# GpSimd raises a constant to a power for 19 score tiles, with the first pair in row order and the final adds on GpSimd

## Chip, cores, metric

One core of a Trainium2 chip. The metric is device microseconds of one execution. Engines are written as in the profile: PE is TensorE, PEld its weight loads, ACT is ScalarE, DVE is VectorE, POOL is GpSimd.

## The reference

Window attention over a 224 x 224 image of 96 channels. Half of the channels attend inside stripes of 8 rows, the other half inside stripes of 8 columns; each stripe has 1792 tokens.

```python
qkv = jnp.einsum('bhwc,cd->bhwd', x, wqkv)
ah = _softmax(jnp.einsum('bqc,bkc->bqk', qh, kh) * scale, axis=-1)   # 28 row stripes
oh = jnp.einsum('bqk,bkc->bqc', ah, vh)
# ... the same for 28 column stripes: ov
o = pad(oh) + pad(ov)
return jnp.einsum('bhwc,cd->bhwd', o, wo)
```

## The kernel before

Stripes are taken in 28 pairs: 14 of rows, then 14 of columns. Each pair has 49 score tiles of 128 x 1024, so 1372 in all, and the exponential of every one is needed. The kernel plans its own order while it is built: `add` keeps a clock for each engine, from estimated durations, and appends an instruction to that engine's list with its semaphore waits. Each engine then runs its list strictly in order.

```python
def add(eng, waits, fn, occ=100.0, done=None):
    cnt[eng] += 1
    ops[eng].append((waits, fn, True))
    start = max([now[0], tfree[eng]] + [vis(w) for w in waits])
    tfree[eng] = start + occ                       # estimate, used only for planning
    ...
```

A tile's exponential is taken in one of two ways. ACT does it in one instruction. DVE does it in five steps, by an approximation; steps 1 to 3 run from SBUF to SBUF:

```python
# ACT tile
e.activation(PTA[sl][:], ps[:, ...], ACTF.Exp, scale=LN2 / 128.0)
# DVE tile
if k == 0: e.tensor_scalar(tt_sb[:], dps.bitcast(U16)[:, 0:2048:2], ..., ALU.mult, ALU.add)  # from PSUM
if k == 1: e.tensor_tensor(sq_sb[:], tt_sb[:], tt_sb[:], ALU.mult)          # square: two SBUF inputs
if k == 2: e.tensor_scalar(sq_sb[:], sq_sb[:], CB, None, ALU.add)           # add constant: SBUF to SBUF
if k == 3: e.tensor_tensor(tt_sb[:], sq_sb[:], tt_sb[:], ALU.mult)          # product: two SBUF inputs
return     e.scalar_tensor_tensor(PTD[sl][:].bitcast(U16), dps, CC, tt_sb[:], ALU.add, ALU.add)
```

K and V of a pair lie in two buffers each (`P % 2`), so the product of a tile with V cannot stand more than about a pair behind its scores. In the column phase DVE also writes each output with one scalar_tensor_tensor per 128 x 96 piece (392 of them).

The softmax here doesn't subtract the row's maximum and nothing guards it: scores larger than these inputs give would overflow.

## Time and profile before

| | before |
|---|---|
| time, median of 3 | 1138.35 us (1138.22 to 1140.09) |
| ACT busy | 1110.5 us, 98% of the span |
| tiles on ACT / DVE | 1200 / 172 |
| first exponential | 17.6 us |

The head of the page, and the shares of the chain of waits by engine:

```profile
span 1137.3 us, 27720 instructions
PE 1023.0 (90%) x11824; PEld 372.9 (33%) x11824; DVE 1088.1 (96%) x2024; ACT 1110.5 (98%) x1206; POOL 1.6 (0%) x9
...
ACT 68%; DVE 20%; PE 9%; SPq 2%; issue 1%; DMA 0%; DVEq 0%
```

ACT is the limit. The groups of the page (count, then busy us and mean ns of one, then idle before them and what ended it):

```profile
L731 ACT ACTIVATE PTA<-ps 128x1024 bf16<-128x1024 f32 x1200 | 1106.6, 1087 | 7.9 <-PE ps L587 6.0
...
L748 DVE TENSOR_TENSOR tt_sb<-sq_sb,tt_sb 128x1024 f16<-128x1024 f16 x172 | 118.5, 689 | 3.6
L744 DVE TENSOR_TENSOR sq_sb<-tt_sb 128x1024 f16<-128x1024 f16 x172 | 117.6, 684 | 0.8
...
L746 DVE TENSOR_SCALAR sq_sb<-sq_sb 128x1024 f16<-128x1024 f16 x172 | 72.2, 420 | 1.6
```

1200 exponentials in 1106.6 us are one per 0.922 us, with 7.9 us idle in front of them. The three DVE lines are the steps square, product and add-constant, 684 to 689 and 420 ns. The timeline of the start (start us, duration us, engine, line, operation; in brackets the idle time before and what ended it):

```profile
12.63 2.08 PE L369 MATMUL ps<-xT_sb,w_sb 96*64 96x448 bf16 x10 [7.82 <-DMA xT_sb<-in_x_dram]
...
17.55 1.94 ACT L731 ACTIVATE PTA<-ps 128x1024 bf16<-128x1024 f32 x2
```

The first product waits for x until 12.6 us, and the first exponential starts at 17.55.

### The profile page before, as it was taken

To read this page: it belongs to the slowest core of one execution; us is meant where nothing else is said; L and a number is where in the kernel's file an instruction comes from. 1 tells how busy PE (TensorE), PEld (TensorE's weight loads), DVE (VectorE), ACT (ScalarE), POOL (GpSimd) and SP (SyncE) were. 2 spreads that over 40 slices of the span, in tenths; PEclk is the share of its full clock that TensorE was granted. 3 is DMA by queue.
4 is the path that set the end of the run, shared out by engine and by line. 5 is a ranking of instruction groups with operands and counts; after the bars stand their busy time and mean duration, and the time that the engine had idled before them with its cause. 6 is when DMAs were issued, how large, how long until landed. Compare 5 with 4: busy or idle time off the path is not lost.

```text
span 1137.3 us, 27720 instructions
## 1 busy us (share of the span) xinstructions
PE 1023.0 (90%) x11824; PEld 372.9 (33%) x11824; DVE 1088.1 (96%) x2024; ACT 1110.5 (98%) x1206; POOL 1.6 (0%) x9
## 2 busy tenths in 40 slices
PE   5898899999999999999998898999899989999987
PEld 1333333333333333333333333333333333333332
DVE  3899999999999999999999999999999999999997
ACT  3999999999999999999999999999999999999998
POOL 0000000000000000000000000000000000000000
PEclk9999999999999999999999999999999999999999
DMA  4311011101100110110111222222122222221111
GB/s 83 54 34 34 10 26 34 34 1 33 35 19 16 33 34 5 30 31 16 21 34 33 40 42 40 38 41 41 38 40 42 40 40 43 40 39 26 19 27 25
DMA packets 169124, 37.31 MB, mean 33 GB/s; under 512 B 169000, under 2 KB 169000, under 8 KB 169000
## 3 DMA queue, kind: packets, MB, share of 16 engines
q1 hardware_dynamic: 167384, 35.36, 16.2%
q8 instruction: 92, 1.51, 0.6%
q10 hardware_dynamic: 1616, 0.18, 0.1%
q14 instruction: 32, 0.26, 0.1%
HBM read 0.15 MB, written 9.63 MB: 9 GB/s over the span
## 4 chain that ended last, share of the span: by engine, by line
ACT 68%; DVE 20%; PE 9%; SPq 2%; issue 1%; DMA 0%; DVEq 0%
ACT PTA L731 68%; PE ps L587 4%; DVE tt_sb L742 4%; PE ps L691 3%; DVE out_sb L521 3%; DVE PTD L749 3%; DVE sq_sb L744 2%; DVE tt_sb L748 2%; SPq L143 2%; DVE QT_sb L396 1%; DVE sq_sb L746 1%; DVE OT_sb L759 1%; DVE KT_sb L420 1%; DVE Ph_sb L482 1%; PE ps L369 1%
## 5 line engine op out<-in xcount | busy, mean ns | idle before, releaser
L731 ACT ACTIVATE PTA<-ps 128x1024 bf16<-128x1024 f32 x1200 | 1106.6, 1087 | 7.9 <-PE ps L587 6.0
L587 PE MATMUL ps<-QT_sb,KT_sb 49*64 49x512 bf16 (+3 forms) x6272 | 540.6, 370 | 81.3 <-ACT PTA L731 71.6
L691 PE MATMUL ps<-PTA,V_sb 128*64 128x512 bf16 (+1 forms) x2734 | 405.4, 365 | 1.4 <-DVE V_sb L337 0.4
L587 PEld LDWEIGHTS ps<-QT_sb,KT_sb 49*64 49x64 bf16 (+1 forms) x6272 | 157.1, 104 | 453.2 <-ACT PTA L731 382.8
L742 DVE TENSOR_SCALAR tt_sb<-ps 128x1024 f16<-128x1024 uint16 x172 | 209.6, 1219 | 12.5 <-PE ps L587 10.8
L749 DVE SCALAR_TENSOR_TENSOR PTD<-ps,tt_sb 128x1024 uint16<-128x1024 f32 x172 | 209.7, 1219 | 1.9
L691 PEld LDWEIGHTS ps<-PTA,V_sb 128*64 128x64 bf16 x2734 | 119.0, 108 | 150.0 <-issue 129.5
L748 DVE TENSOR_TENSOR tt_sb<-sq_sb,tt_sb 128x1024 f16<-128x1024 f16 x172 | 118.5, 689 | 3.6
L744 DVE TENSOR_TENSOR sq_sb<-tt_sb 128x1024 f16<-128x1024 f16 x172 | 117.6, 684 | 0.8
L369 PE MATMUL ps<-xT_sb,w_sb 128*64 128x448 bf16 (+1 forms) x448 | 85.5, 381 | 18.6 <-DMA xT_sb<-in_x_dram 9.9
L521 DVE SCALAR_TENSOR_TENSOR out_sb<-ps,rc,Ph_sb 128x96 bf16<-128x96 f32 x392 | 96.8, 308 | 1.0
L746 DVE TENSOR_SCALAR sq_sb<-sq_sb 128x1024 f16<-128x1024 f16 x172 | 72.2, 420 | 1.6
L396 DVE TENSOR_SCALAR QT_sb<-ps,biasq 128x448 bf16<-128x448 f32 x108 | 73.0, 676 | 0.4
L759 DVE CAST OT_sb<-ps 128x512 bf16<-128x512 f32 x112 | 68.9, 616 | 3.5 <-PE ps L691 3.5
L691 PE MATMUL ps<-PTD,V_sb 128*64 128x512 bf16 (+1 forms) x402 | 66.8, 353 | 2.7 <-DVE QT_sb L396 2.3
L420 DVE TENSOR_SCALAR KT_sb<-ps,shift 128x448 bf16<-128x448 f32 x84 | 56.6, 676 | 1.8 <-PE ps L369 1.6
L337 DVE CAST V_sb<-ps 128x480 bf16<-128x480 f32 (+1 forms) x84 | 51.5, 615 | 2.2 <-PE ps L330 2.2
L482 DVE TENSOR_TENSOR Ph_sb<-ps,rc 128x480 bf16<-128x480 f32 x84 | 52.0, 619 | 1.1
L369 PEld LDWEIGHTS ps<-xT_sb,w_sb 128*64 128x64 bf16 (+1 forms) x448 | 25.3, 108 | 72.5 <-issue 25.6
L471 PE MATMUL ps<-wo_sb,OT_sb 128*64 128x97 bf16 x784 | 33.0, 212 | 2.5 <-DMA wo_sb<-one_sb 1.6
L510 PE MATMUL ps<-wo_sb,OT_sb 128*128 128x97 bf16 x392 | 32.9, 210 | 2.2 <-DVE OT_sb L759 1.2
L330 PE MATMUL ps<-w_sb,xT_sb 128*128 128x48 bf16 (+1 forms) x784 | 34.1, 185 | 0.7 <-DVE V_sb L337 0.4
(33 smaller groups left out, 168.1 us busy)
## 6 DMA issues: line engine op xcount, KB each, us to landing
out_dram<-out_sb SPq DMA_DIRECT2D x389, 24.0 KB, 1.9
xT_sb<-in_x_dram SPq DMA_TRANSPOSE x336, 2.5
w_sb<-in_wqkv_dram ACTq DMA_DIRECT2D x2, 54.0 KB, 2.9
out_dram<-out_sb ACTq DMA_DIRECT2D x3, 24.0 KB, 1.9
wo_sb<-in_wo_dram SPq DMA_DIRECT2D x4, 9.0 KB
wo_sb<-one_sb SPq DMA_DIRECT2D x4, 0.0 KB
```

The lines of the kernel that those rows point to most:

```text
L369: ins = e.matmul(o, lhsT=wS[0:kr, wblk(P, kind), :], rhs=x_cols(wdw), start=True, stop=True)
L396: return e.tensor_scalar(q_dst, q_src(bk), QS, biasq[:, 0:1], ALU.mult, ALU.add)
L521: return e.scalar_tensor_tensor(out_sb[b][:, wdw, k0 + s, :], bk3[:, s, 0:C], rci[:, s:s + 1], Ph_sb[:, k0 + s, j, :], ALU.mult, ALU.add)
L587: ins = e.matmul(bank(base + wdw)[64 * kh:64 * kh + 64, i * qs:(i + 1) * qs], lhsT=KT_sb[b][r0:r0 + kk, kt * 128 + 64 * kh:kt * 128 + 64 * ...
L691: ins = e.matmul(bk[64 * wdw:64 * wdw + 64, 0:qs], lhsT=V_sb[b][:, wdw, kt, :], rhs=pt[:, wdw * 512 + i * qs:wdw * 512 + (i + 1) * qs], st ...
L731: e = add("act", [ev, bufA_ev[sl]], lambda e, base=base, sl=sl: e.activation(PTA[sl][:], ps[:, base * 512:(base + 2) * 512], ACTF.Exp, sca ...
L742: return lambda e: e.tensor_scalar(tt_sb[:], dps.bitcast(U16)[:, 0:2048:2], CS / 65536.0, CS * CA3, ALU.mult, ALU.add)
L744: return lambda e: e.tensor_tensor(sq_sb[:], tt_sb[:], tt_sb[:], ALU.mult)
L746: return lambda e: e.tensor_scalar(sq_sb[:], sq_sb[:], CB, None, ALU.add)
L748: return lambda e: e.tensor_tensor(tt_sb[:], sq_sb[:], tt_sb[:], ALU.mult)
L749: return lambda e: e.scalar_tensor_tensor(PTD[sl][:].bitcast(U16), dps, CC, tt_sb[:], ALU.add, ALU.add)
L759: ev = add("dve", [e_pv], lambda e: e.tensor_copy(OT_sb[b][:, q0:q0 + qs], bank(bi)[:, 0:qs]), t_ps(qs), t_ps(qs) + 150.0)
```

## The change

Its intent: start sooner (the first pair in row order, with x and the weights loaded so that work begins after 512 columns), take the final adds of the column phase from DVE to GpSimd, and give GpSimd some score tiles. GpSimd raises 2^(1/128) to the score, which is the same exponential. DVE first copies the tile from PSUM to SBUF. The core of the diff, cut, with remarks that name the place:

```diff
+    NPT = 400
+    TPOW = 25000.0                       # reserved for one power, ns
+        PTP = [sb(f"PTP{i}", [128, 1024], BF16) for i in range(NBP)]
+        zp_sb = [sb(f"zp_sb{i}", [128, 1024], FP32) for i in range(NZP)]
+        e_base = add("dve", [], lambda e: e.memset(base_sb[:], 2.0 ** (1.0 / 128.0)))
...
+            # pick_pe: choose a tile far enough ahead for a 25 us power
+                lo = max(progress(), lastA[0]) + int(TPOW / 770.0) + 4
+                for G in range(min(lo + 12, NGTOT - 6), lo - 1, -1):
...
+            # do_d: the copy from PSUM
+                ev = add("dve", [d["prev"], zp_rd[0]], lambda e: e.tensor_copy(zp_sb[0][:], dps), D_OCC[0], D_OCC[0] + 80.0)
...
+            # pick_pool
+                    e = add("pool", [ev, bufP_ev[sl], e_base], lambda e, sl=sl: e.tensor_tensor(
+                        PTP[sl][:], base_sb[:].to_broadcast([128, 1024]), zp_sb[0][:], ALU.pow), TPOW)
...
-                    def mk_d(s):          # 392 DVE output steps
-                            return e.scalar_tensor_tensor(out_sb[b][:, wdw, k0 + s, :], bk3[:, s, 0:C], rci[:, s:s + 1],
-                                                          Ph_sb[:, k0 + s, j, :], ALU.mult, ALU.add)
+                    def d2(e, bk):        # multiply on DVE, for up to five pieces at once
+                    def d3(e):            # add on GpSimd, placed by a gate on DVE's position
```

The rest (cut here) changes the lead-in, the planner's figures (for example ACT 904 ns a tile instead of 912), and adds a few idle-time products that are meant to keep PE's clock up. The built program has 1188 tiles on ACT, 165 on DVE and 19 on GpSimd.

## The prediction

> **What bounds the kernel now.** ScalarE. The page gives ACT 1110.5 us busy of 1137.3 (98%), DVE 96%, PE 90%. The groups view: 1200 exponentials of 128x1024, 1106.6 us in all, so one every 0.922 us, with only 7.9 us idle before them. The timeline: first exponential at 17.6 us (x lands at 12.6), about 4 us of gaps until 26 us, then back to back until 1132; tail 5 to 6 us. So only fewer exponentials or an earlier start help.
>
> **What the change does** (order of the built programs):
> 1. ACT tiles 1200 -> 1188, DVE tiles 172 -> 165, and 19 new GpSimd tiles. ACT: -12 x 0.922 = -11 us, all on the critical path.
> 2. Lead-in: row-order first pair, weights' DMA issued before the table load, the first 512 columns loaded alone. A transposing load is issued every 1.35 us (32.4 us for 24), so the first product needs 2 loads instead of 8: estimate 6-7 us instead of 12.6. First exponential near 9 us, some lost again to the remaining columns. Estimate -10 us, critical.
> 3. The 392 DVE output steps (96.8 us) become multiplies (about 0.62 us for five, as the 128x480 ones: some 55 us) and GpSimd adds. DVE: -42 us, -7 x 4.23 = -30 us for DVE tiles, +19 x 1.22 = +23 us for copies out of PSUM. DVE holds 20% of the chain; I take this as slack.
>
> Steps 1 and 2 alone: 1138 - 21 = about 1117 us.
>
> 4. The 19 powers of 128x1024. No trace shows one; the source reserves 25 us each. Their products stand 32 to 170 exponentials later in the program (34 x 0.922 = 31 us at the tight ones): latency alone should stall nobody. The port can. The Trainium skill ("SBUF — State Buffer", section "Who interferes with whom") says GpSimd and DVE share one port pair as an exclusive lock for a whole instruction, and that DVE operations with two SBUF inputs or in a two-port mode block on it. Each DVE tile has three such steps in a row (square 684 ns, add constant 420, product 689). The before trace has only a hint: a 128x128 conversion of DVE took 441 ns while GpSimd memsets ran, and ended just after them. If the lock holds through a compute-heavy power, DVE stops 2-3 us after each power starts, and stands for about 22 us; PE, in order, meets a DVE result 3-6 us later, and ACT with its two PSUM pairs starves. Net 16-20 us per power, 19 x 18 = 342 us, plus a slow PE after each pause.
>
> I hold the lock for likelier (about 70%): about 1440-1470 us. If the port is free while GpSimd computes: 1108-1130 us. Shared in pieces: between.
>
> **What would show it.** Lock: DVE square, add-constant or product steps lasting up to 20+ us, one or two per power; GpSimd busy near 475 us; ACT idle some 15-20 us after each power, tiles still 0.922 apart otherwise. No lock: those steps keep 684/420/689 ns, ACT 97-98% busy, span 1110-1125. Lead-in: first exponential at 8-10 us. Step 1: 1188 x 0.922 = 1095 us ACT busy.
>
> **What would make it wrong.** A power that lets the port go between pieces or is far shorter than 25 us; powers over 31 us (then waits for them even without a lock); PE, ordered with tighter estimates, becoming the limit.
>
> I predict 1440 us, range 1108 to 1530; faster by over 2% 0.14, within 2% 0.17, slower by over 2% 0.69.

## The result, and the profile after

| | before | after |
|---|---|---|
| median | 1139.22 us (4 runs) | 4240.19 us (4 runs, 4221.28 to 4247.91) |
| ratio | | 3.719 (95%: 3.705 to 3.733) |
| ACT busy | 1110.5 us (98%) | 1117.0 us (26%) |
| POOL busy | 1.6 us | 3197.4 us (75%) |

Ratios are the mean time of one kernel's fast runs over that of the other's of the same rounds, so not quite the ratio of the medians quoted. The times of before quoted with later runs are those of the same rounds and differ by about a microsecond.

The head of the page of after, two rows of its 40 slices (busy tenths of ACT, and PE's granted clock in tenths), and its chain of waits:

```profile
span 4246.1 us, 27634 instructions
PE 1169.2 (28%) x11837; PEld 389.2 (9%) x11837; DVE 4089.9 (96%) x1722; ACT 1117.0 (26%) x1191; POOL 3197.4 (75%) x117
...
ACT  1113990303030703051303030303030303030318
...
PEclk5556995656565856575656565656565656565658
...
DVE 74%; ACT 15%; PE 9%; issue 2%; DMA 0%; SPq 0%
DVE sq_sb L840 34%; DVE sq_sb L842 34%; ACT PTA L827 15%; PE ps L660 4%; PE ps L788 4%; DVE KT_sb L464 2%; DVE tt_sb L838 1%; PE ps L419 1%; DVE PTD L845 1%; DVE zp_sb L928 0%; DVE tt_sb L844 0%; PE ps L563 0%; DVE tmp L575 0%; DVE Ph_sb L535 0%; DVE OT_sb L872 0%
```

The chain has moved from ACT to DVE, to two lines, L840 (square) and L842 (add-constant), at 34% each. After the first quarter ACT's row alternates between 0 and mostly 3 (at most 7, and 8 in the last slice), and PE's granted clock is near half in most slices. The groups:

```profile
L913 POOL TENSOR_TENSOR PTP<-base_sb,zp_sb 128x1024 bf16<-128x1024 f32 x19 | 3101.2, 163221 | 547.5 <-DVE zp_sb L928 547.3
L827 ACT ACTIVATE PTA<-ps 128x1024 bf16<-128x1024 f32 x1188 | 1114.8, 1156 | 3113.4 <-PE ps L660 3110.8
L840 DVE TENSOR_TENSOR sq_sb<-tt_sb 128x1024 f16<-128x1024 f16 x165 | 1634.7, 9907 | 0.2
L842 DVE TENSOR_SCALAR sq_sb<-sq_sb 128x1024 f16<-128x1024 f16 x165 | 1504.9, 9121 | 2.5
...
L844 DVE TENSOR_TENSOR tt_sb<-sq_sb,tt_sb 128x1024 f16<-128x1024 f16 x165 | 113.3, 686 | 3.3
```

One power takes 163.2 us, not 25. Between exponentials ACT stands for 3113 us in all, and 19 x 163.2 = 3101. ACT's own work is within 2% of what was expected (1188 x 0.922 = 1095 us, here 1115). The mean of the square has risen from 684 to 9907 ns and that of add-constant from 420 to 9121, while the product (L844) is unchanged (689 before, 686 now). One power from near by: first GpSimd, then DVE, then PE, from their timelines.

```profile
631.99 163.21 POOL L913 TENSOR_TENSOR PTP<-base_sb,zp_sb 128x1024 bf16<-128x1024 f32 x1 [250.09 <-DVE zp_sb L928]
```

```profile
630.69 1.23 DVE L928 COPY zp_sb<-ps 128x1024 f32<-128x1024 f32 x1 [0.19 <-PE ps L660]
...
633.87 80.98 DVE L840 TENSOR_TENSOR sq_sb<-tt_sb 128x1024 f16<-128x1024 f16 x1
714.78 0.65 DVE L535 TENSOR_TENSOR Ph_sb<-ps,rc 128x480 bf16<-128x480 f32 x1
715.35 80.14 DVE L842 TENSOR_SCALAR sq_sb<-sq_sb 128x1024 f16<-128x1024 f16 x1
795.52 0.69 DVE L844 TENSOR_TENSOR tt_sb<-sq_sb,tt_sb 128x1024 f16<-128x1024 f16 x1
```

```profile
715.48 0.62 PE L524 MATMUL ps<-wo_sb,OT_sb 128*64 128x97 bf16 x10 [80.30 <-DVE Ph_sb L535]
```

The copy into SBUF ends at 631.9 and the power starts. DVE's next square starts at 633.9 and stays for 80.98 us; one operation out of PSUM goes through; then the add-constant stays for 80.14 us, and ends when the power ends (631.99 + 163.21 = 795.20). The product after it runs in its usual 0.69 us. PE issues its last work at 634.8 and then, as its line says, waits 80.30 us for a DVE result. The other 18 powers look the same: each holds one two-input step for about 80 us and then one SBUF-to-SBUF step to its end (in the first power that second step is a shift of K, L464). The same stretch in windows (busy us of PE, PEld, DVE, ACT and POOL with instruction counts, then PE's granted clock, DMA share, GB/s):

```profile
636.00:715.00 79.00, 0.00 (x0) 0.00 (x0) 79.00 (x2) 0.15 (x1) 79.00 (x1) 0.51 0.03 4
715.00:796.00 81.00, 3.90 (x28) 1.14 (x28) 80.97 (x3) 3.07 (x3) 80.21 (x1) 0.50 0.00 0
```

In the 160 us from 636 to 796 ACT does 3.2 us of work.

The start went as predicted: the first product at 6.0 us and the first exponential at 8.4 us.

```profile
6.03 0.62 PE L419 MATMUL ps<-xT_sb,w_sb 96*64 96x512 bf16 x4
...
8.42 1.94 ACT L827 ACTIVATE PTA<-ps 128x1024 bf16<-128x1024 f32 x2 [1.04 <-PE ps L660]
```

### The profile page after: what moved, and what is told of

Its sections match the earlier page's. It is cut to its first block, busy times and chain, and to the rows that moved or that the text cites. A ratio compares the mean times of both kernels' runs of the same rounds, so it can differ in the third digit from the quotient of the medians.

```text
span 4246.1 us, 27634 instructions
## 1 busy us (share of the span) xinstructions
PE 1169.2 (28%) x11837; PEld 389.2 (9%) x11837; DVE 4089.9 (96%) x1722; ACT 1117.0 (26%) x1191; POOL 3197.4 (75%) x117
## 4 chain that ended last, share of the span: by engine, by line
DVE 74%; ACT 15%; PE 9%; issue 2%; DMA 0%; SPq 0%
DVE sq_sb L840 34%; DVE sq_sb L842 34%; ACT PTA L827 15%; PE ps L660 4%; PE ps L788 4%; DVE KT_sb L464 2%; DVE tt_sb L838 1%; PE ps L419 1%; DVE PTD L845 1%; DVE zp_sb L928 0%; DVE tt_sb L844 0%; PE ps L563 0%; DVE tmp L575 0%; DVE Ph_sb L535 0%; DVE OT_sb L872 0%
## 5 line engine op out<-in xcount | busy, mean ns | idle before, releaser
L913 POOL TENSOR_TENSOR PTP<-base_sb,zp_sb 128x1024 bf16<-128x1024 f32 x19 | 3101.2, 163221 | 547.5 <-DVE zp_sb L928 547.3
L840 DVE TENSOR_TENSOR sq_sb<-tt_sb 128x1024 f16<-128x1024 f16 x165 | 1634.7, 9907 | 0.2
L842 DVE TENSOR_SCALAR sq_sb<-sq_sb 128x1024 f16<-128x1024 f16 x165 | 1504.9, 9121 | 2.5
L788 PE MATMUL ps<-PTA,V_sb 128*64 128x512 bf16 (+1 forms) x2690 | 479.8, 414 | 715.1 <-DVE tmp L575 399.0
L598 POOL TENSOR_TENSOR out_sb<-tmp,Ph_sb 128x480 bf16<-128x480 f32 (+2 forms) x89 | 94.5, 1076 | 490.4 <-DVE PTD L845 130.4
L419 PE MATMUL ps<-xT_sb,w_sb 128*64 128x448 bf16 (+3 forms) x448 | 96.1, 425 | 477.8 <-DVE OT_sb L872 237.0
L844 DVE TENSOR_TENSOR tt_sb<-sq_sb,tt_sb 128x1024 f16<-128x1024 f16 x165 | 113.3, 686 | 3.3
L464 DVE TENSOR_SCALAR KT_sb<-KT_sb,shift 128x448 bf16<-128x448 bf16 (+1 forms) x28 | 89.4, 3193 | 0.1
L449 DVE TENSOR_SCALAR QT_sb<-ps,biasq 128x448 bf16<-128x448 f32 (+2 forms) x111 | 75.1, 677 | 9.4 <-PE ps L419 9.1
L524 PEld LDWEIGHTS ps<-wo_sb,OT_sb 128*64 128x64 bf16 x784 | 24.9, 117 | 580.2 <-DVE OT_sb L872 482.4
L872 DVE CAST OT_sb<-ps 128x512 bf16<-128x512 f32 (+5 forms) x118 | 69.2, 591 | 8.7 <-PE ps L788 8.5
L473 DVE TENSOR_SCALAR KT_sb<-ps,shift 128x448 bf16<-128x448 f32 (+2 forms) x84 | 56.8, 677 | 18.3 <-PE ps L419 18.3
```

Source lines behind the costliest of these rows:

```text
L419: ins = e.matmul(o, lhsT=wS[0:kr, wblk(P, kind), :], rhs=x_cols(wdw), start=True, stop=True)
L464: return e.tensor_scalar(KT_sb[b][:, q0:q0 + qs], KT_sb[b][:, q0:q0 + qs], shift[b][:, 0:1], None, ALU.add)
L598: return e.tensor_tensor(out_sb[b][:, wdw, k0:k0 + n, :], tmpi[:, 0:n, :], Ph_sb[:, k0:k0 + n, j, :], ALU.add)
L788: ins = e.matmul(bk[64 * wdw:64 * wdw + 64, 0:qs], lhsT=V_sb[b][:, wdw, kt, :], rhs=pt[:, wdw * 512 + i * qs:wdw * 512 + (i + 1) * qs], st ...
L840: return lambda e: e.tensor_tensor(sq_sb[:], tt_sb[:], tt_sb[:], ALU.mult)
L842: return lambda e: e.tensor_scalar(sq_sb[:], sq_sb[:], CB, None, ALU.add)
```

## The experiments

Three causes could each make a power expensive: DVE is held up by it ("port"); its result comes 163 us after the start while the program placed the product 31 us or more behind ("lateness"); or something else in the change is slow.

### 1. No powers: `NPT = 0`

```diff
-    NPT = 400
+    NPT = 0
```

> Everything of the change except the powers (their number set to 0; the scheduler then gives 1201 tiles to ScalarE and 171 to VectorE). If the powers are the whole of the loss, this takes the kernel before less the lead-in: about 1139 - 9 = 1130 us (1122 to 1134), ScalarE idle below 12 us after its first ten tiles, and no VectorE square or add-constant over 1 us. If the row order, the GpSimd adds or the tighter scheduler figures cost something too, it is above 1139 us.

Measured: 1135.69 us against 1139.07, ratio 0.996 (0.994 to 0.998). On balance the rest of the change does not cost anything, so the powers are the whole of the loss. No DVE square or add-constant took more than 0.70 us. The gain is smaller than expected; see the end of the next experiment.

### 2. A multiply in the place of each power

```diff
-                        PTP[sl][:], base_sb[:].to_broadcast([128, 1024]), zp_sb[0][:], ALU.pow), TPOW)
+                        PTP[sl][:], base_sb[:].to_broadcast([128, 1024]), zp_sb[0][:], ALU.mult), TPOW)
```

> Same program, order and waits as the changed kernel, but each of the 19 GpSimd operations multiplies instead of raising to a power (the result is wrong on purpose). If only the duration of the power hurts, each takes about 2.6 us (1.09 us for 480 columns, scaled to 1024), VectorE is blocked 0 to 2 us each, and the time is about 1117 us (1112 to 1130). If the schedule itself, the copies out of PSUM or the 19 extra dependences hurt, it stays far above 1139 us.

Measured: 1128.28 us against 1139.07, ratio 0.991 (0.988 to 0.994); the result is wrong, as intended. Program order, waits, copies and counts are those of the changed kernel. From its groups:

```profile
L842 DVE TENSOR_SCALAR sq_sb<-sq_sb 128x1024 f16<-128x1024 f16 x165 | 69.6, 422 | 2.5
...
L913 POOL TENSOR_TENSOR PTP<-base_sb,zp_sb 128x1024 bf16<-128x1024 f32 x19 | 36.0, 1892 | 532.4 <-DVE zp_sb L928 532.1
```

So order, copies and dependences are harmless, and the difference from the changed kernel is the operation alone: (4240 - 1128) / 19 = 163.8 us lost per power, its whole duration.

This run also shows what steps 1 and 2 of the prediction were worth: not 21 us but 11 to 12. Of the traces' spans (1137.3 and 1125.2 us), the exponentials are 1106.6 and 1092.6 us busy (-14), the first starts at 17.55 and 8.30 (-9.3), but the idle time between them is 7.9 and 12.8 us (the 13.8 us of its group less the 1.0 before the first; +4.9), and from the last one to the end it is 5.2 and 11.5 us (+6.3). The windows of mult (busy us of PE, PEld, DVE, ACT and POOL with counts, then PE's granted clock, DMA share, GB/s) show where part of the new idle time lies:

```profile
12.00:18.00 6.00, 5.73 (x37) 1.17 (x29) 4.24 (x8) 4.90 (x5) 0.00 (x0) 0.50 0.46 95
18.00:24.00 6.00, 6.00 (x36) 1.33 (x36) 2.96 (x4) 4.09 (x4) 0.00 (x0) 0.50 0.37 77
138.00:152.00 14.00, 14.00 (x102) 3.48 (x98) 7.44 (x11) 9.74 (x11) 0.00 (x0) 0.54 0.20 42
```

PE's granted clock is half there though PE is recorded busy throughout, and ACT does 4.90 and 4.09 us of work in 6, and 9.74 in 14. In the kernel before the same three windows have a clock of 1.00, and ACT is busy 14.00 us in the last (in the first two that kernel is still in its lead-in, with 2.85 and 3.43 us). Why the clock drops there was not tested. The longer tail was not tested either.

### 3. A power that does last 25 us: 154 columns

```diff
-                        PTP[sl][:], base_sb[:].to_broadcast([128, 1024]), zp_sb[0][:], ALU.pow), TPOW)
+                        PTP[sl][:, 0:PCOL], base_sb[:].to_broadcast([128, PCOL]), zp_sb[0][:, 0:PCOL], ALU.pow), TPOW)   # PCOL = 154
```

The columns left out are set once at the start.

> The power over 154 of the 1024 columns only, about 24.6 us each by 163.2 us / 1024, which is the 25 us that the source reserves (wrong result on purpose). Port theory: VectorE's square stands still for about 20 us per power, ScalarE loses 14 to 20 us each, 19 of them make 270 to 380 us: 1390 to 1500 us, as the prediction had it for its own assumption. Latency theory (only late results hurt): products stand 31 us or more after, so nothing is lost: about 1117 us.

Measured: 1126.32 us against 1139.07, ratio 0.989 (0.985 to 0.993). My port theory, as I had put it, fell: the powers took the 24.9 us that the source reserves, no DVE square took more than 1.25 us and no add-constant more than 0.43, and nothing was lost against the multiply. (The square of 1.25 us stood beside one of GpSimd's adds, not beside a power.)

```profile
L916 POOL TENSOR_TENSOR PTP<-base_sb,zp_sb 128x154 bf16<-128x154 f32 x19 | 472.7, 24879 | 364.5 <-DVE zp_sb L931 364.3
L843 DVE TENSOR_TENSOR sq_sb<-tt_sb 128x1024 f16<-128x1024 f16 x165 | 113.5, 688 | 0.2
...
L845 DVE TENSOR_SCALAR sq_sb<-sq_sb 128x1024 f16<-128x1024 f16 x165 | 69.5, 421 | 2.5
```

So a power does not hold the port merely because it runs. This run shortens the power and narrows it at once, so it does not say what a power of 1024 columns in 25 us would do. Experiments 4 to 9 look for what the 1024 columns do.

### 4. Three powers that nobody reads

To separate the port from lateness, the kernel of experiment 1 gets three powers of 1024 columns on a constant tile, into a tile nobody reads:

```diff
...
+        for gate in (62, 162, 262):       # started when ACT has done 60, 160, 260 tiles
+            side(gate, lambda e: e.tensor_tensor(PTP[0][:], base_sb[:].to_broadcast([128, 1024]), zp_sb[0][:], ALU.pow))
```

> The kernel without powers, plus three powers of 128x1024 that read a constant tile and write a tile nobody reads, started when ScalarE has done 60, 160 and 260 tiles. No engine waits for them by data. Port theory: about 1130 + 3 x 160 = 1610 us, with two VectorE operations of about 80 us in each. Latency theory (PE stands for the late result): no change, about 1130 us, since GpSimd has no other work in that half.

Measured: 1625.7 us (2 runs), or (1625.7 - 1135.7) / 3 = 163.3 us per power. Nothing waits for these powers by data, so GpSimd's hold on DVE is enough for the whole loss (that it needs DVE's SBUF-to-SBUF steps is shown by experiment 5). The shape was not as expected, though: here DVE happened to reach the add-constant first in all three powers, and that one operation stood to the end of the power. From DVE's timeline (L849 is add-constant; the product after it took 0.69 us):

```profile
69.68 163.46 DVE L849 TENSOR_SCALAR sq_sb<-sq_sb 128x1024 f16<-128x1024 f16 x1
```

### 5. The same without contending DVE operations

Control: no DVE tiles at all, and the one other SBUF-to-SBUF operation (shift of the first K piece) reads PSUM instead.

```diff
+    DVE_TILES = False
...
-  return e.tensor_scalar(KT_sb[b][:, q0:q0 + qs], KT_sb[b][:, q0:q0 + qs], shift[b][:, 0:1], None, ALU.add)
+  return e.tensor_scalar(KT_sb[b][:, q0:q0 + qs], bk[:, 0:qs], shift[b][:, 0:1], None, ALU.add)
```

> Control for the next two: no powers, no VectorE tiles (ScalarE takes all 1372), and the first K piece is shifted from PSUM, so that no VectorE operation in the row phase has two SBUF inputs or a fast SBUF-to-SBUF mode. Both theories: 1372 x 0.922 + about 20 = 1285 us (1275 to 1310).

Measured: 1281.69 us. With three unread powers of 1024 columns:

> The control plus the same three unread powers as in side3. Port theory, with only those VectorE operations contending that read two SBUF tiles or run SBUF to SBUF: no loss, within 1% of the control. If a power blocks every VectorE operation, or slows the core in another way: about +480 us.

Measured: 1282.65 us. Three powers, back to back, cost nothing. GpSimd's and ACT's timelines:

```profile
75.38 489.95 POOL L220 TENSOR_TENSOR PTP<-base_sb,zp_sb 128x1024 bf16<-128x1024 f32 x3 [72.24 <-ACT PTA L835]
```

```profile
69.40 501.81 ACT L835 ACTIVATE PTA<-ps 128x1024 bf16<-128x1024 f32 x547
```

547 exponentials run without a gap across all three. DVE operations that read PSUM were not held by these powers (324 of them overlapped one, none took over 0.70 us); in experiment 4 the SBUF-to-SBUF ones were. This agrees with the section of the Trainium skill that the prediction names ("SBUF — State Buffer", "Who interferes with whom"): a DVE operation with at most one SBUF input, outside the two-port modes, does not contend with GpSimd.

### 6. Lateness alone

The control of experiment 5 with three powers whose results are used (`NPT = 3`, still planned at 25 us):

> The control with three powers whose results are used, under the scheduler's 25 us. There is no contending VectorE operation here, so this shows what the late result alone costs: a power of 163 us whose product the program places 33 to 45 us later leaves 115 to 130 us of standing each, about 1285 - 3 + 3 x 122 = 1650 us, with PE waiting for GpSimd in the trace. If lateness costs nothing: about 1282 us.

Measured: 1694.12 us, or (1694.1 - 1281.7) / 3 = 137 us per power, without any contention for the port. The list of waits names it (in all, times, longest):

```profile
DVE zp_sb L929 <- POOL PTP L914: 276.2, 2, 139.8
...
PE ps L789 <- POOL PTP L914: 263.6, 2, 134.9
```

PE stands for GpSimd's result, and DVE's next copy stands for the tile that the power still reads. There is one such tile, and the three powers run almost end to end from 24.4 to 516.9 us, so the 137 us hold both waits that a late power causes; in experiment 9 the wait for the result alone makes up nearly all.

### 7. How size matters

Nine unread GpSimd operations, one at a time, in the kernel of experiment 1.

```diff
+        side(62, lambda e: e.tensor_tensor(PTP[0][:, 0:256], bc(256), big[:, 0:256], ALU.pow))
+        side(112, ... 512 columns) ; side(162, ... 768) ; side(212, ... 2048) ; side(262, ... 2048, ALU.mult)
...
```

> The kernel without powers plus nine unread GpSimd operations, one at a time: powers of 256, 512, 768 and 2048 columns, a multiply of 2048 and of 1024, a power of 512 columns on 64 partitions, one with a bf16 exponent, and a multiply by a scalar. If a power costs a fixed time per column, 40.8, 81.6, 122.4 and 326.4 us. If the port is let go after every 512 columns, VectorE is blocked once by 256 and 512, twice by 768 (about 80 and 40 us) and four times about 80 us by 2048; if it is let go at half of any instruction, twice each (20, 41, 61 and 163 us). Multiplies about 5 and 2.6 us. 64 partitions: the same time as 128[...].

GpSimd's timeline:

```profile
114.50 81.92 POOL L225 TENSOR_TENSOR PTP<-base_sb,big 128x512 bf16<-128x512 f32 x1 [4.68 <-ACT PTA L847]
196.57 122.63 POOL L226 TENSOR_TENSOR PTP<-base_sb,big 128x768 bf16<-128x768 f32 x1
334.50 325.82 POOL L227 TENSOR_TENSOR bigo<-base_sb,big 128x2048 bf16<-128x2048 f32 x1 [15.30 <-ACT PTA L847]
707.73 3.65 POOL L228 TENSOR_TENSOR bigo<-base_sb,big 128x2048 bf16<-128x2048 f32 x1 [47.41 <-ACT PTA L847]
```

A power costs 159 ns a column (325.82 / 2048). 64 partitions take as long as 128 (81.98 against 81.92 us for 512 columns). DVE's, in the powers of 512 and of 2048 columns (L860 square, L862 add-constant):

```profile
116.43 0.68 DVE L860 TENSOR_TENSOR sq_sb<-tt_sb 128x1024 f16<-128x1024 f16 x1
...
117.63 0.41 DVE L862 TENSOR_SCALAR sq_sb<-sq_sb 128x1024 f16<-128x1024 f16 x1
...
334.83 245.15 DVE L860 TENSOR_TENSOR sq_sb<-tt_sb 128x1024 f16<-128x1024 f16 x1
580.01 80.59 DVE L862 TENSOR_SCALAR sq_sb<-sq_sb 128x1024 f16<-128x1024 f16 x1
```

Powers of 256 and 512 columns hold nothing: the square and add-constant in the middle of the second one take 0.68 and 0.41 us. (The one operation that met the start of the 256-column power, an add-constant, took 0.85 us.) The power of 768 held the square until 82.4 us after its start and the next add-constant to its end. The power of 2048 held the square for 245.15 us, three quarters of its time, and the add-constant for the last quarter. Neither of the two rules I had written down fits: it is not let go after every 512 columns, nor at half. What fits these sizes, as a reading that no run shows directly, is that GpSimd computes in pieces of 512 columns, that a two-input operation is held until the last piece begins, and that an add-constant is held to the end.

The same run also tells columns from duration. The multiply of 2048 columns lasted only 3.65 us, and yet held an add-constant to its end:

```profile
708.17 3.49 DVE L862 TENSOR_SCALAR sq_sb<-sq_sb 128x1024 f16<-128x1024 f16 x1
```

The multiply of 1024 columns (2.07 us) held one for 1.75 us, while a power of 512 columns lets steps through for 81.92 us. So how long an instruction lasts does not decide whether it holds DVE.

The whole run took 1586.91 us. With odd sizes:

> The kernel without powers plus three unread powers: 520 columns, 1024 columns with a bf16 exponent (2 KB a partition, as 512 of fp32), 640 columns. Durations 82.9, 163.2 and 102 us. If the limit is 512 elements, all three block: at least 81 us each for the first two-input operation, to the end for a fast-mode one. If the limit is 2 KB of the exponent, the bf16 one blocks nobody and the other two do.

Measured, once (1395.59 us in all): 83.4, 163.2 and 102.8 us. From the timelines of GpSimd and DVE (L856 add-constant):

```profile
69.45 83.37 POOL L224 TENSOR_TENSOR PTP<-base_sb,big 128x520 bf16<-128x520 f32 x1 [63.43 <-ACT PTA L841]
```

```profile
324.61 102.44 DVE L856 TENSOR_SCALAR sq_sb<-sq_sb 128x1024 f16<-128x1024 f16 x1
```

The power of 520 columns held nothing beyond a 1.29 us operation at its start; the one with a bf16 exponent held a DVE operation for 160.2 us, to its end, and the one of 640 columns held one for 102.4 us, to its end. So for powers the size that matters is the number of columns, not the exponent's bytes, and the limit lies between 520 and 640, not at exactly 512. By the reading above, 520 columns would make a second piece of 8 columns, and that piece held nothing; so the reading is not complete.

### 8. Is the reading side let go before the end?

The kernel of experiment 4 with only two-input operations on DVE:

```diff
...
-  return lambda e: e.tensor_scalar(sq_sb[:], sq_sb[:], CB, None, ALU.add)
+  return lambda e: e.tensor_tensor(sq_sb[:], sq_sb[:], cb_sb[:], ALU.add)
```

(and the K shift from PSUM, as in experiment 5)

> As side3 (three unread powers of 1024 columns), but VectorE adds its constant from a tile (two SBUF inputs) instead of in the fast SBUF-to-SBUF mode, and the first K piece is shifted from PSUM, so only operations with two SBUF inputs contend. Theory R: the reading side is free once the last 512 columns are read, the writing side is held from the first to the last write; then each power blocks one VectorE operation for about 81 us and the second half runs freely: about 1140 + 3 x 78 = 1375 us (1340 to 1420). Theory W: the whole port is held to the end, apart from one operation that slips through at the middle: two blocks of 80 us, about 1620 us.

Measured, once: 1464.25 us, 90 us over theory R. DVE's timeline in the first power, which ran from 70.70 to 233.93 us (L849 square, L851 constant added from a tile, L853 product):

```profile
72.15 81.43 DVE L849 TENSOR_TENSOR sq_sb<-tt_sb 128x1024 f16<-128x1024 f16 x1
...
154.07 0.67 DVE L851 TENSOR_TENSOR sq_sb<-sq_sb,cb_sb 128x1024 f16<-128x1024 f16 x1
154.78 0.69 DVE L853 TENSOR_TENSOR tt_sb<-sq_sb,tt_sb 128x1024 f16<-128x1024 f16 x1
```

One block of 81 us, then two-input steps at normal speed inside the second half of the power (the next tile's square too, 0.68 us at 159.86); the same in the other two powers (79.1 and 81.3 us). To find the owner of the 90 us, the control without powers was run:

> Control for tt_side3: the same kernel (VectorE adds its constant from a tile, K piece shifted from PSUM) without the three powers. tt_side3 took 1464 us where its theory R had 1375. If theory R is right and the missing control explains the miss, this takes 1464 - 3 x 80 = about 1220 us, with ScalarE gaps of about 2 us per pair as in tt_side3. If it takes about 1140 us, each power cost 108 us, more than the one block of 81 us, and theory R lacks something.

Measured, once: 1218.68 us. So the altered DVE steps cost 83 of the 90 us (1218.68 - 1135.69), and the three powers (1464.25 - 1218.68) / 3 = 81.9 us each, half a power. What theory R says of two-input steps holds, and W falls; no two-input step was held past the middle.

### 9. Powers cut in two

First unread, as experiment 4 but with two instructions of 512 columns for each power:

> As side3, but each of the three unread powers as two instructions of 512 columns. If the port is held only by instructions of more than 512 columns: no loss, 1130 to 1140 us against 1626 for side3. If a power holds it whatever its size: about 1626 us.

Measured: 1135.46 us (2 runs), that of no powers at all (1135.69), against 1625.7 uncut. The same arithmetic, the same 163.8 us of GpSimd, and no loss; the longest add-constant took 1.27 us and the longest square 1.00, each at the start of a half.

Then in the changed kernel itself:

```diff
-                    e = add("pool", [ev, bufP_ev[sl], e_base], ... [128, 1024] ... ALU.pow), TPOW)
+                    for h in range(2):
+                        e = add("pool", [ev, bufP_ev[sl], e_base], ... columns 512 * h to 512 * h + 512 ... ALU.pow), TPOW / 2)
```

> The changed kernel with each power cut into two instructions of 512 columns (correct result, same places in the program, 19 of them). In the sizes run a power of 512 columns let every VectorE operation through. If the held port were the only cause, this takes what the multiply took, about 1128 us. If the late result alone is enough, each of the 19 still leaves PE standing: nod_pow3 showed 137 us each, and the products stand 31 us or more behind, so about 1128 + 19 x 130 = 3600 us (3300 to 3750), with PE waiting for GpSimd and no VectorE operation over 2 us.

Measured: 3670.18 us (2 runs), correct. The longest DVE square is now 1.05 us, and no power holds DVE any more. One add-constant stood for 4.11 us beside four of GpSimd's adds in a row (at most 480 columns, about 1 us each). So narrow instructions can hold DVE too while they run; that a power of 512 columns holds almost nothing is not a rule for every operation of that width. Still (3670 - 1128) / 19 = 133.8 us are lost per power, and the list of waits names lateness:

```profile
ACT PTA L827 <- PE ps L660: 2537.3, 141, 138.2
...
PE ps L788 <- POOL PTP L914: 2329.1, 18, 133.9
```

### Which version is best

Of the correct versions the one without powers (experiment 1) is the fastest, 0.4% below the kernel before; at the margin of 2% used here that counts as the same. Powers could not add much: at 159 ns a column GpSimd could raise some 6900 columns in 1100 us, or 6.7 tiles, worth 6.2 us of ACT before the copies. This is an estimate from the measured durations.

## Why the prediction was wrong

- **What bounds the kernel** (ACT, 0.922 us a tile): right. With the power made short, the exponentials make up 1092.6 of 1125.2 us.
- **Steps 1 and 2, "about 1117 us"**: mechanism right (first product 6.0 us, first exponential 8.3 to 9.1 us, 1188 tiles), but half was given back: 1128 us, by +4.9 us of idle time between exponentials and +6.3 us of tail in the traces.
- **Step 3** (DVE relieved): right. Its busy time was to fall by 49 us to 1039; it is 1047.9 in mult.
- **Step 4, "the source reserves 25 us each"**: the step that failed. I took a planner's constant for a duration because no trace had one, and let my range rest on it. The power takes 163.2 us, 6.5 times as much. I gave a longer power as what would make the prediction wrong, but only over 31 us and without a size. The sum with the right term, 1128 + 19 x 163.2 = 4229 us (the time with a multiply, and every power lost whole), is within 0.3% of the measured 4240.
- **Step 4, the port as "exclusive lock for a whole instruction"**: right in what it does at 1024 columns, where DVE's SBUF-to-SBUF steps stood, PE met a DVE result within 3 us and ACT starved. It was wrong as a general rule. A power of 154 columns, at just the 25 us that I assumed, held nothing and lost nothing: 1126 us where I had expected 1390 to 1500 for it. Even a 163 us power as two instructions of 512 columns loses nothing when nobody waits for it. So "slower", held at 0.69, came true partly by luck: for a power of the 25 us assumed, made of 154 columns, the loss of 16 to 20 us that the sum charged to the port was not there.
- **"Latency alone should stall nobody"**: wrong for the same reason as the 25 us. At the real duration it costs 134 us per power by itself (split19), so there are two causes. Either alone costs most of each power's 163 us (all of it by the port in side3, 134 us by lateness in split19), and removing one leaves the other. A third bound stands behind both: 19 x 163.2 us of GpSimd work is 3.1 ms, however it is hidden.

What is shown: the duration, the loss per power, that the hold on DVE's SBUF-to-SBUF steps and lateness each cost most of it alone, which DVE operations are held and until when. What is only argued: that DVE's two-input steps wait for the reading side (GpSimd reads until its last piece is in) and its fast SBUF-to-SBUF steps also for the writing side. That picture fits the long blocks in the traces, but no run looks at the port itself. Why 520 columns pass and 640 do not is open, as is why four narrow adds could hold one step for 4.11 us, and so are the slow clock and the longer tail in mult.

## What to carry to other kernels

A constant in a planner is a wish until a trace shows the duration; before building a schedule around an operation that no trace has, run that operation once by itself, unread, and read its span. When two causes can each explain a loss, build a run for each that leaves only that one: an operation whose result nobody reads shows contention, and the operation without contending neighbours shows lateness. A long GpSimd instruction that must run beside SBUF-to-SBUF work on DVE can be cut into short ones: here two of 512 columns held DVE for less than 1 us each where one of 1024 held it from start to end. Cutting helps only if the result is not waited for: in the changed kernel it still left 134 us lost per power.

## What the Trainium skill lacked or had wrong

- "SBUF — State Buffer", section "Who interferes with whom", has the shared pair as an exclusive lock, held "for the whole instruction" against DVE's two-port modes, and has two-input operations contend with GpSimd's reads. Here the whole instruction holds for fast SBUF-to-SBUF operations beside powers of 640 columns and more (163.46 us of a 163.2 us power) and multiplies of 1024 and 2048 columns (1.75 of 2.07 us, 3.49 of 3.65 us). It does not hold for powers of 154 to 520 columns, which held DVE for no more than about 1 us of their 24.9 to 83.4 us, nor for two-input operations, which were let through after half of a 1024-column power (81.4 of 163.2 us) and three quarters of a 2048-column one (245 of 326 us).
- No page that I found gives the cost of a power on GpSimd: 159 ns a column here, about 70 times an add. For an add, "GPSIMD Engine Reference", section "3.1 Elementwise — side-by-side cycle accounting", gives 4497 ns for 2048 columns (2.2 ns a column); the 480-column add here took 1.09 us (2.3 ns a column), which agrees.
- "Perfetto Trace Analysis", section "GPSIMD Engine Instruction", calls GpSimd spans unreliable and advises timing by spacing. For these powers the span was as good as the spacing: three powers back to back took 489.95 us, 163.3 each, and the recorded span of one is 163.2 us.
- "TensorE: Matmul & The Clock Gate", Part 1, has the clock released after about 3.4 us of sustained activity. In mult it stayed at 0.50 from 12 to 24 us while PE was recorded busy for 11.7 of those 12 us (and at 0.50 to 0.51 in the runs without powers and with 154 columns). This is a hint, not a refutation: PE's recorded busy time is modelled, and why the clock stayed low was not tested.
